# Windowed attention with a routed FFN: values as they lie in memory, 128x64 tiles, and a list planner for the order

## The chip, the cores and the metric

One core of a Trainium2 chip runs the whole program. The metric is the device time of one execution in microseconds. Before the change it is 393.38 us, the median of three runs (390.45 to 393.67).

## The reference

Batch 8, 8 heads, 576 positions, head size 64. Heads 0 to 3 see the last 32 positions, heads 4 to 7 every fourth of the last 128. The joined heads are x of a routed FFN: in each batch the 128 positions with the highest gate score go through a two-layer FFN and get its result added.

```python
scores = scale * np.matmul(q, k.transpose(0, 1, 3, 2))
mask_plain = (rel >= 0) & (rel < window)                                        # window 32
mask_dil = (rel >= 0) & (rel < window * dilation) & (rel % dilation == 0)       # dilation 4
attn = np.exp(scores - max) ; attn = attn / (sum + 1e-09)
x = np.matmul(attn, v)                                # heads joined: 576 x 512 for each batch
...
scores = np.einsum('bsd,d->bs', x, w_gate)
top_idx = np.argpartition(-scores[b], capacity)[:capacity]                      # capacity 128
ye = np.maximum(xe @ w1, 0.0) @ w2                                              # 512 -> 1024 -> 512
out[b, top_idx] = x[b, top_idx] + g[:, None] * ye                               # g: sigmoid of the score
```

## The kernel before

A batch is five units (`UNITS`, line 36): p0 and p1 are 256 positions of the plain heads, d0 and d1 256 of the dilated heads, and l the 64 last positions of both. Queries are grouped by 32; each group sees 64 keys (48 in the dilated half of l). A unit goes through these steps:

1. `scores` (141): 16 matmuls on tiles of 128 rows by 32 columns, 12 in l. A matmul takes two heads at once: queries and keys of two heads lie one under the other in the partitions, and the keys are laid out with zeros so that the heads stay apart. The trace counts each float32 matmul as two instructions, so 32 a unit.
2. `maximum` (153, VectorE): adds the mask, finds the maximum of each head, and subtracts it.
3. `transposes` (176): four 128x128 transposes into one PSUM bank, tile t.
4. `weights` (187, ScalarE): one exponential of 128 x 512 into tile pt.
5. `attend` (197): 16 matmuls (12 in l) again on 128x32 tiles, 130 value columns each, two heads at once. For this the values vp, vd and vl lie in SBUF with zeros between the heads.
6. `normalise` (210): the reciprocal of the sum on VectorE, then the division on ScalarE (8 instructions) or VectorE (1); `store` (234) writes x to memory, `gate` (252, VectorE) takes its dot product with the gate vector.

After a batch's last unit comes the routing: `order` and `spread` (286, 294) add the two halves of the score on TensorE and VectorE and spread them over all partitions; `rank` and `mark` (305, 314, VectorE) count for each position how many are better and mark its slot; `pick` (323) gets the indices by matmul, and POOL fetches the 128 rows by an indirect DMA. `experts` (341) is the FFN: 48 matmuls of 512 columns (three to a product, with both sides split in a rounded part and a rest), turns by TensorE between the layers, and an indirect DMA that writes the rows back. The FFN weights are split in the same way at the start, ScalarE rounding and POOL subtracting (`split_weights`, 276), through four buffers `raw`.

The order is written out in a loop (491 to 533). Iteration g issues the value products of unit g - 2, the scores of g, the division and store of g - 2, the transposes and exponentials of g - 1, half of the iteration's FFN pieces (three or four, `rate`), `maximum` of g and `gate` of g - 2, the routing steps that fall due, and the other FFN pieces. Loads stand at the iteration's end on SP's queue: queries and keys of the next batch behind the scores that read them last, and values of the next batch behind the value products that read them last,

```python
        if 0 <= g - 2 < total and b + 1 < B:
            if u == 2:
                load_vp(b + 1)
                load_vl(b + 1)
            if u == 4:
                load_vd(b + 1)
```

since vp, vd and vl have one buffer each, as have queries and keys. PSUM's eight banks: two for scores (s), one for transposes (t), two for a unit's products (a), three for all the rest (m).

Of the kernel before, what the change touches and what calls it, by code (L numbers as in the profile page):

```python
# [9 lines left out]
F32 = mybir.dt.float32  # L10
# [30 lines left out]
    xd=4,  # L41
    xe=6,
    w1=(2, 4), w2=(7, 9),
    per=2,
    rate=(3, 4, 4),
)


@with_exitstack
def tile_window_attention_moe(ctx, tc, qt, kt, va, vb, w_gate, w1, w2, masks, mask_l, ident, slots, toks, outs, capacity):  # L50
# [6 lines left out]
    ctx.enter_context(tc.manual_schedule())  # L57


    id32 = cp.tile([P, P], F32, name="id32")  # L60
    perm = cp.tile([P, P], F32, name="perm")
# [3 lines left out]
    mkl = cp.tile([P, 2 * LK], BF16, name="mkl")  # L65
# [7 lines left out]
    vp = cp.tile([P, 18, 2, 2 * (D + 1)], F32, name="vp")  # L73
    vd = cp.tile([P, 4, 4, 2, 2 * (D + 1)], F32, name="vd")
    vl = cp.tile([P, 4, 2, 2 * (D + 1)], F32, name="vl")
# [5 lines left out]
    raw = {}  # L81
# [15 lines left out]
    def load_vp(b, lo=0, hi=9):  # L97
        for h in range(2):
            for u in range(2):
                src = va[b, u * GK:(u + 1) * GK, 4 * VW:13 * VW].rearrange("k (c h f) -> k c h f", c=9, h=2)  # L100
                nc.sync.dma_start(  # L101
                    out=vp[h * GK:(h + 1) * GK, 2 * lo:2 * hi].rearrange("k (c u) h f -> k c u h f", u=2)[:, :, u, h],
                    in_=src[:, lo:hi, h])

    def load_vd(b):
        for j in range(4):
            n = GK if j < 3 else G
            for h in range(2):
                src = va[b, G * j:G * j + n, 0:4 * VW].rearrange("k (r h f) -> k r h f", r=4, h=2)[:, :, h]
                nc.sync.dma_start(out=vd[h * GK:h * GK + n, 3 - j, :, h], in_=src)  # L110

    def load_vl(b):
        for h in range(2):
            for i in range(2):
                src = vb[b, i * LK:(i + 1) * LK].rearrange("k (e h f) -> k e h f", e=2, h=2)[:, :, h]
                nc.sync.dma_start(out=vl[h * LK:(h + 1) * LK].rearrange("k (e i) h f -> k e i h f", i=2)[:, :, i, h],  # L116
                                  in_=src)
# [6 lines left out]
    def window(kind, s, c, w):  # L124

        if kind == "p":
            g = 8 * s + 4 * c + w
            return qs[0], G * g, ks[0], G * g, GK, vp[:, g]
        if kind == "l":
            if c:  # L130
                return window("p", 2, 0, w)
            return qs[1], 4 * P + 16 * w, ks[1], SR * w, LK, vl[0:2 * LK, w]
        j = 2 * s + c
        return qs[1], P * w + G * j, ks[1], SR * w + SR - G * (j + 1), GK, vd[:, j, w]

    def chunks(kind):

        return ((4, P, LK, 0), (2, HB, GK, 4 * LK)) if kind == "l" else ((4, P, GK, 0), (4, P, GK, 4 * GK))


    def scores(g):
        kind, s = UNITS[g % NU]
        st = ps.tile([P, 512], F32, tag="s", bufs=2, name=f"s_{g}")
        for c, (nw, rows, wid, o) in enumerate(chunks(kind)):
            for p in range(2):
                for w in range(nw):
                    q, q0, k, k0, _, _ = window(kind, s, c, w)
                    out = st[G * w:G * (w + 1), o + 2 * p * wid:o + 2 * (p + 1) * wid]
                    nc.tensor.matmul(out.rearrange("q (h k) -> q h k", h=2), q[:, p, q0:q0 + G],  # L149
                                     k[:, p, :, k0:k0 + wid], start=True, stop=True)  # L150
        return st

    def maximum(g, st):
        kind, s = UNITS[g % NU]
        ms = wk.tile([P, 512], F32, tag="ms", bufs=3, name=f"ms_{g}")
        mx = wk.tile([P, 8], F32, tag="mx", bufs=3, name=f"mx_{g}")
        for c, (nw, rows, wid, o) in enumerate(chunks(kind)):
            first = s == c == 0
            m = {"p": (mk0 if first else mk)[:, GK:2 * GK], "d": (mk0 if first else mk)[:, 0:GK],
                 "l": mk[:, GK:2 * GK] if c else mkl[:, 0:LK]}[kind]  # L160
            for w in range(4):
                cols = slice(o + w * wid, o + (w + 1) * wid)
                nc.vector.tensor_tensor_reduce(  # L163
                    out=ms[:rows, cols], in0=st[:rows, cols], in1=m[:rows], scale=1.0, scalar=-3.0e38,
                    op0=ALU.add, op1=ALU.max, accum_out=mx[:rows, 4 * c + w:4 * c + w + 1])
        parts = chunks(kind) if kind == "l" else ((8, P, GK, 0),)
        i = 0
        for nw, rows, wid, o in parts:
            n = max(nw, 4)
            v = ms[:rows, o:o + n * wid].rearrange("q (u k) -> q u k", u=n)  # L170
            nc.vector.tensor_tensor(  # L171
                out=v, in0=v, in1=mx[:rows, i:i + n].unsqueeze(2).to_broadcast([rows, n, wid]), op=ALU.subtract)
            i += n
        return ms

    def transposes(g, dt):
        kind, s = UNITS[g % NU]
        tt = ps.tile([P, 512], F32, tag="t", bufs=1, name=f"t_{g}")
        for c, (nw, rows, wid, o) in enumerate(chunks(kind)):
            for p in range(2):  # L180
                t0 = 256 * c + p * rows
                nc.tensor.transpose(tt[:2 * wid, t0:t0 + rows], dt[:rows, o + 2 * p * wid:o + 2 * (p + 1) * wid],  # L182
# [429 lines left out]
```

## Time and profile before

| | |
|---|---|
| time, median of three runs | 393.38 us |
| the profiled execution | 391.99 us, span 390.3 us, mean granted clock 0.85 |
| TensorE busy (matmuls; weight loads) | 276.3 us, 71% of the span; 211.9 us |
| VectorE, ScalarE, POOL busy | 211.7, 107.1, 53.5 us |
| chain that ended last, by engine | PE 34%, DMA 19%, SP's queue 15%, issue 13%, DVE 13% |
| its largest lines | value load vp 12%, value products (line 206) 10%, py (389) 6%, ph (374) 6%, scores (149) 6% |
| value loads of a batch | vp 4 DMAs of 292.5 KB, vd 8 of 130 or 65 KB, vl 4 of 48.8 KB |

PE is TensorE, PEld its weight loads, DVE VectorE, ACT ScalarE, SPq the queue of SyncE, from which nearly all DMAs are issued. The granted clock is a share of 2.4 GHz; the chip knows 2.4 and 1.2 GHz, so a mean of 0.85 is a mixture of both. A line's idle time is that of the engine just before it, with what ended it. Matmuls overlap, so the time from one start to the next tells more than the length of one.

### The profile page before, as it was taken

What the parts mean: (1) busy time and instruction counts of PE and PEld (TensorE: products, weight loads), DVE (VectorE), ACT (ScalarE), POOL (GpSimd) and SP (SyncE); (2) the same over time, 40 slices, a digit from 0 to 9 for tenths busy, and PEclk for the clock granted to TensorE, in tenths of its full rate; (3) what the DMA queues carried; (4) which work ended last, traced back from release to release, by engine and by line L of the source; (5) the groups of instructions that cost most, each with busy time, mean ns of one, the idle gap of its engine ahead of it and who ended that gap; (6) DMA issues with size and microseconds to landing.
All of it is one profiled execution on the core that took longest, in us unless ns stands there. A gap on an engine that the chain in (4) does not pass through costs nothing.

```text
span 390.3 us, 8755 instructions
## 1 busy us (share of the span) xinstructions
PE 276.3 (71%) x3193; PEld 211.9 (54%) x3193; DVE 211.7 (54%) x1173; ACT 107.1 (27%) x346; POOL 53.5 (14%) x59
## 2 busy tenths in 40 slices
PE   6658255596579756796679866795679956788794
PEld 3546144484457555574457654564557644566573
DVE  2439728673574807565384716656384726654631
ACT  1012204343323222241323321241232421252120
POOL 9612502242200100010000100010000100010011
PEclk9997758687688988899688986899888986898999
DMA  7988987789822968259741968149561974112000
GB/s 171 223 207 253 219 182 189 230 223 203 212 67 56 235 124 205 71 154 188 181 111 42 242 134 210 61 117 210 131 178 39 223 141 110 54 39 59 28 27 27
DMA packets 62203, 56.37 MB, mean 144 GB/s; under 512 B 5840, under 2 KB 52176, under 8 KB 62160
## 3 DMA queue, kind: packets, MB, share of 16 engines
q1 hardware_dynamic: 60448, 51.49, 56.8%
q0 software_dynamic: 1280, 4.20, 3.4%
q8 instruction: 25, 0.41, 0.4%
q10 hardware_dynamic: 432, 0.12, 0.2%
q14 instruction: 18, 0.15, 0.1%
HBM read 44.26 MB, written 11.53 MB: 143 GB/s over the span
## 4 chain that ended last, share of the span: by engine, by line
PE 34%; DMA 19%; SPq 15%; issue 13%; DVE 13%; POOL 2%; ACT 2%; POOLq 0%; DVEq 0%
DMA vp<-in_va_dram 12%; PE a L206 10%; PE py L389 6%; PE ph L374 6%; PE s L149 6%; SPq L101 5%; DMA out_dram<-x 4%; SPq L94 3%; DVE ms L163 3%; SPq L116 3%; PE t L182 2%; DVE junk L262 2%; DVE junk L310 2%; DVE ms L171 2%; PE pht L382 2%
## 5 line engine op out<-in xcount | busy, mean ns | idle before, releaser
L230 ACT ACTIVATE x<-a,rin 128x64 f32<-128x64 f32 (+1 forms) x216 | 46.9, 325 | 95.3 <-DVE rin L220 62.9
L206 PE MATMUL a<-vp,pt 128*32 128x130 f32 x576 | 37.5, 370 | 38.6 <-DMA vp<-in_va_dram 22.0
L149 PE MATMUL s<-ks,qs 128*32 128x128 f32 (+1 forms) x1216 | 58.0, 316 | 4.7 <-DMA ks<-in_kt_dram 4.7
L206 PEld LDWEIGHTS a<-vp,pt 128*32 128x32 f32 x576 | 27.3, 149 | 49.3 <-issue 38.6
L149 PEld LDWEIGHTS s<-ks,qs 128*32 128x32 f32 x1216 | 48.3, 130 | 6.9 <-issue 5.4
L163 DVE CUSTOM_DVE_ANT_0 ms<-s,mk 128x64 f32<-128x64 f32 (+1 forms) x288 | 44.5, 218 | 12.1 <-PE s L149 12.1
L262 DVE CUSTOM_DVE_ANT_0 junk<-x,wg 128x256 bf16<-128x256 f32 x80 | 38.4, 480 | 9.3 <-DMA wg<-in_gate_dram 6.2
L218 DVE TENSOR_SCALAR den<-a 128x8 f32<-128x8 f32 (+2 forms) x48 | 7.0, 159 | 62.7 <-PE a L206 62.7
L310 DVE SCALAR_TENSOR_TENSOR junk<-sb,sc,thr_sb 128x576 bf16<-128x576 f32 (+1 forms) x40 | 33.0, 826 | 13.3 <-ACT sb L302 13.3
L192 ACT ACTIVATE pt<-t 128x512 f32<-128x512 f32 (+2 forms) x48 | 24.0, 522 | 53.8 <-PE t L182 53.8
L374 PE MATMUL ph<-w1h,xh 128*128 128x512 f32 x64 | 31.9, 499 | 6.0 <-ACT xh L347 6.0
L336 POOL DMA_INDIRECT xe<-out_dram,ix x8 | 7.9, 991 | 196.8 <-DVE ix L332 196.8
L348 DVE TENSOR_TENSOR hl<-pht,hh 128x512 fp32r<-128x512 f32 x16 | 11.1, 692 | 41.5 <-ACT hh L347 41.5
L182 PE MATMUL t<-id,ms 128*128 128x128 f32 (+2 forms) x160 | 30.7, 318 | 0.2 <-DVE ms L171 0.2
L171 DVE TENSOR_TENSOR ms<-ms,mx 128x512 f32<-128x512 f32 (+2 forms) x48 | 29.6, 630 | 1.1
L389 PE MATMUL py<-w2h,hh 128*128 128x512 f32 x64 | 29.2, 456 | 0.0
L374 PE MATMUL ph<-w1h,xl 128*128 128x512 f32 x64 | 29.0, 453 | 0.0
L374 PE MATMUL ph<-w1l,xh 128*128 128x512 f32 x64 | 28.3, 443 | 0.0
L300 PE MATMUL pa<-id,sc 128*128 128x128 f32 (+1 forms) x40 | 9.0, 351 | 25.5 <-DVE sc L292 25.5
L389 PE MATMUL py<-w2h,hl 128*128 128x512 f32 x64 | 26.5, 414 | 0.0
L389 PE MATMUL py<-w2l,hh 128*128 128x512 f32 x64 | 26.5, 414 | 0.0
L163 DVE DVE_READ_ACCUMULATOR2_ANT mx<- 128x1 f32 (+1 forms) x320 | 26.3, 82 | 0.0
(77 smaller groups left out, 362.4 us busy)
## 6 DMA issues: line engine op xcount, KB each, us to landing
qs<-in_qt_dram SPq DMA_DIRECT2D x15, 576.0 KB, 6.4
ks<-in_kt_dram SPq DMA_DIRECT2D x30, 288.0 KB, 7.1
vp<-in_va_dram SPq DMA_DIRECT2D x28, 292.5 KB, 9.1
vd<-in_va_dram SPq DMA_DIRECT2D x48, 130.0 KB, 3.3
out_dram<-x SPq DMA_DIRECT2D x72, 64.0 KB, 2.8
out_dram<-x SPq DMA_DIRECT2D x16, 256.0 KB, 2.9
raw<-in_w_dram SPq DMA_DIRECT2D x16, 256.0 KB, 3.8
vl<-in_vb_dram SPq DMA_DIRECT2D x32, 48.8 KB, 6.2
```

What stands on the lines that cost most here:

```text
L101: nc.sync.dma_start(out=vp[h * GK:(h + 1) * GK, 2 * lo:2 * hi].rearrange("k (c u) h f -> k c u h f", u=2)[:, :, u, h], in_=src[:, lo:hi, h])
L149: nc.tensor.matmul(out.rearrange("q (h k) -> q h k", h=2), q[:, p, q0:q0 + G], k[:, p, :, k0:k0 + wid], start=True, stop=True)
L163: nc.vector.tensor_tensor_reduce(out=ms[:rows, cols], in0=st[:rows, cols], in1=m[:rows], scale=1.0, scalar=-3.0e38, op0=ALU.add, op1=ALU.m ...
L171: nc.vector.tensor_tensor(out=v, in0=v, in1=mx[:rows, i:i + n].unsqueeze(2).to_broadcast([rows, n, wid]), op=ALU.subtract)
L182: nc.tensor.transpose(tt[:2 * wid, t0:t0 + rows], dt[:rows, o + 2 * p * wid:o + 2 * (p + 1) * wid], id32[:rows, :rows])
L192: nc.scalar.activation(pt[:n, lo:hi], tt[:n, lo:hi], AF.Exp, scale=SCALE)
L206: nc.tensor.matmul(out, pt[:2 * wid, t0:t0 + G], v.rearrange("k h (p f) -> k h p f", p=2)[:, :, p], start=True, stop=True)
L230: nc.scalar.activation(x[:n, c, h, :], av[:n, c, h, 0:D], AF.Copy, scale=rin[:n, c, h:h + 1])
L262: nc.vector.tensor_tensor_reduce(out=junk[:n], in0=x[:n, c].rearrange("q h d -> q (h d)"), in1=wg[:n, 256 * dil:256 * (dil + 1)], scale=UP ...
L310: nc.vector.scalar_tensor_tensor(out=junk[:n], in0=st["sb"][:n], scalar=st["sc"][:n, t:t + 1], in1=thr_sb[:n, o:o + S], op0=ALU.subtract, ...
L374: nc.tensor.matmul(e["ph"], x[:, i, :], w[:, i, n * 512:(n + 1) * 512], start=i == 0 and k == 0, stop=i == 3 and k == 2)
L389: nc.tensor.matmul(e["py"], x[:, i, :], w[:, i, :], start=i == 0 and k == 0, stop=i == 7 and k == 2)
```

## The change

**Values and their products.** The values keep their layout in memory: a row of 260 numbers holds four heads with a one behind each. vp, vd and vl get two buffers each, chosen by the batch's parity. Where a tile of keys serves two query groups, the transposed weights get the zeros: `pts` are three buffers whose zero parts are written once at the start, and an exponential now is four instructions of 64 partitions x 256, each into its part. A product is then 128 keys by 64 queries (a 128x64 tile) for one head and 65 columns.

```diff
     def load_vp(b, lo=0, hi=9):
-        for h in range(2):
-            for u in range(2):
-                src = va[b, u * GK:(u + 1) * GK, 4 * VW:13 * VW].rearrange("k (c h f) -> k c h f", c=9, h=2)
-                nc.sync.dma_start(
-                    out=vp[h * GK:(h + 1) * GK, 2 * lo:2 * hi].rearrange("k (c u) h f -> k c u h f", u=2)[:, :, u, h],
-                    in_=src[:, lo:hi, h])
+        nc.sync.dma_start(out=vp[b % 2][:, lo:hi].rearrange("k c f -> k (c f)"), in_=va[b, :, (4 + lo) * VW:(4 + hi) * VW])
...
-            nc.scalar.activation(pt[:n, lo:hi], tt[:n, lo:hi], AF.Exp, scale=SCALE)
...
+        for u in range(2):
+            for h in range(2):
...
+                nc.scalar.activation(pts[g % 3][GK * u:GK * (u + 1), 2 * h:2 * h + 2, 0:n, u], src, AF.Exp, scale=SCALE)
...
-                    nc.tensor.matmul(out, pt[:2 * wid, t0:t0 + G],
-                                     v.rearrange("k h (p f) -> k h p f", p=2)[:, :, p], start=True, stop=True)
...
+        for y in range(3 if kind == "l" else 4):
...
+            for h in range(4):
+                f = slice(h * (D + 1), (h + 1) * (D + 1))
+                nc.tensor.matmul(at[HB * (y % 2):HB * (y % 2 + 1), y // 2, f],
+                                 pts[g % 3][:, h, y].rearrange("k u q -> k (u q)"), v[:, f], start=True, stop=True)
```

The dilated positions now stand in another order in x, so a store of d is two DMAs and not four, and `order` adds the halves with five matmuls and not two. In unit l all scores have 64 columns.

**Order.** Each step becomes an entry with its engine, a fixed cost in us, the entries that it needs, a due time, the tile size of TensorE, and the buffers that it takes and frees. The planner takes, again and again, the engine that can start first, and on it, among the entries that could start within 0.05 us of the first, the one due earliest; TensorE pays 1.5 us of due time for another tile size. What is written into the program is the order alone.

```diff
+        while n:
+            best = None
+            for eng, ws in ready.items():
...
+                first = min(t for t, _ in cands)
+                t, w = min(((t, w) for t, w in cands if t <= first + 0.05),
+                           key=lambda c: (c[1].due + (self.penalty if c[1].mode not in (None, mode) else 0.0), c[1].n))
+                if best is None or t < best[0]:
+                    best = (t, w)
...
+            v_in[b, "p"] = A("SP", 0.4, lambda b=b: (load_vp(b), load_vl(b)), [old[0], v_in[b - 1, "p"]], d - 8, lag=8.0)
...
+        att[g] = A("PE", 0.75 if kind == "l" else 0.98, lambda g=g: attend(g), [e, v_in[b, "d" if kind == "d" else "p"]],
+                   d + 6, mode=64, takes=[("a", g)], lag=0.1)
...
+        by_vector = g % T["xv"] == 0
```

Here `old[0]` is the last product that read the same buffer, two batches back. Every second unit is divided on VectorE, where it was 13 of 40. A batch's FFN is due 15 us behind its routing. The work ahead of the first unit (masks, zeros, tables) is not known to the planner.

Where rows moved. **SP's queue, second to fourth batch** (L101, L116 and L110 load values, L87 and L94 queries and keys, L239 to L248 store). Before:

```order
L239 DMA out_dram<-x_1118 128x2x256
L87 DMA qs_77<-in_qt_dram 128x1152
L94 DMA ks_79<-in_kt_dram 64x2x576 x2
L239 DMA out_dram<-x_1239 128x2x256
L246 DMA out_dram<-x_1339 64x256
L248 DMA out_dram<-x_1339 16x256 x4
L87 DMA qs_78<-in_qt_dram 128x2x576
L94 DMA ks_80<-in_kt_dram 64x2x576 x2
L101 DMA vp<-in_va_dram 64x9x130 x4
L116 DMA vl<-in_vb_dram 48x2x130 x4
```

And in the change (L199 and L209 load values, L188 and L195 queries and keys):

```order
L342 DMA out_dram<-x_1727 128x2x256
L188 DMA qs_77<-in_qt_dram 128x1152
L195 DMA ks_79<-in_kt_dram 64x2x576 x2
L342 DMA out_dram<-x_1936 128x2x256
L199 DMA vp_82<-in_va_dram 128x2340
L209 DMA vl_86<-in_vb_dram 48x520 x2
L188 DMA qs_78<-in_qt_dram 128x2x576
L195 DMA ks_80<-in_kt_dram 64x2x576 x2
L349 DMA out_dram<-x_2017 64x256
L351 DMA out_dram<-x_2017 16x256 x4
```

The value load of p and l has moved ahead of the second query and key load and of unit l's store, and it now fills a buffer that is read a batch later.

**ACT's queue at the start** (L192 and L288 are exponentials, L282 and L384 round FFN weights, L334 divides). Before:

```order
L192 ACTIVATE pt_216<-t_211 128x512
L192 ACTIVATE pt_271<-t_266 128x512
L192 ACTIVATE pt_347<-t_342 96x256
L192 ACTIVATE pt_347<-t_342 128x128
L192 ACTIVATE pt_418<-t_413 128x512
L282 CAST w1h<-raw_294 128x512
L282 CAST w1h<-raw_296 128x512
L192 ACTIVATE pt_503<-t_498 128x512
```

And in the change:

```order
L384 CAST w1h<-raw_163 128x512
L384 CAST w1h<-raw_165 128x512
L384 CAST w1h<-raw_167 128x512
L384 CAST w1h<-raw_169 128x512
L288 ACTIVATE pt_87<-t_241 64x8x32 x4
L384 CAST w1h<-raw_194 128x512
L288 ACTIVATE pt_88<-t_255 64x8x32 x4
L384 CAST w1h<-raw_224 128x512
L384 CAST w1h<-raw_246 128x512
L384 CAST w1h<-raw_253 128x512
L334 ACTIVATE x_406<-a_338,rin_399 128x64 x8
L288 ACTIVATE pt_89<-t_392 64x2x3x32 x4
```

The first exponentials stood ahead of all weight casts; now four casts stand ahead of the first, and eight ahead of the third.

**TensorE around a routing** (pg is the sum of the scores' halves, pa their spread, ph, pht and py the FFN, a value products, s scores, t transposes). Before:

```order
L374 MATMUL ph_0_1_1579<-w1h,xl_0_1472 128x512
L382 MATMUL pht_0_0_1645<-id_66,h_0_1499 128x128 x4
L289 MATMUL pg_1673<-sd_1157,perm 128x4
L290 MATMUL pg_1673<-sd_1157,perml 64x1
L300 MATMUL pa_0_1678<-id_66,sc_1158 128x128 x4
L300 MATMUL pa_4_1684<-id_66,sc_1158 128x64
L374 MATMUL ph_0_1_1579<-w1h,xh_0_1471 128x512
...
L206 MATMUL a_1707<-vp,pt_1640 32x2x65 x16
L149 MATMUL s_1724<-ks_80,qs_78 32x128 x16
```

And in the change:

```order
L398 MATMUL pg_2302<-sd_1912,perm 128x2 x4
L399 MATMUL pg_2302<-sd_1912,perml 64x1
L512 MATMUL ph_0_0_2248<-w1h,xh_0_2201 128x512
L512 MATMUL ph_0_0_2248<-w1l,xh_0_2201 128x512
L512 MATMUL ph_0_0_2248<-w1h,xl_0_2202 128x512
L274 MATMUL t_2318<-id_66,ms_2073 128x128 x4
L412 MATMUL pa_0_2340<-id_66,sc_1913 128x128 x4
L412 MATMUL pa_1_2341<-id_66,sc_1913 128x64
...
L239 MATMUL s_2360<-ks_80,qs_78 32x128 x16
...
L305 MATMUL a_2394<-vl_85,pt_88 64x65 x8
```

Between pg and pa, which needs pg's sum from VectorE, stand an FFN piece and a unit's transposes where nothing stood; products and scores are no longer next to each other.

## Rows read from the trace of the kernel before

**Rows 1.** Waits of TensorE: in all, how often, the longest (us)
```profile
PE pa L300 <- DVE sc L292: 25.5, 8, 4.6
PE pi L330 <- DVE oh L319: 23.8, 18, 4.0
PE a L206 <- DMA vp<-in_va_dram: 22.0, 9, 4.6
PE a L206 <- DMA out_dram<-x: 15.1, 4, 11.7
```

**Rows 2.** The chain that ended last, one batch: start, length, what
```profile
125.33 0.61 SPq L94
...
128.85 11.43 DMA vp<-in_va_dram
...
140.41 1.69 PE a L206 x25
```

**Rows 3.** Stretches: length, busy PE, PEld, DVE, ACT, POOL, clock, DMA, GB/s
```profile
228.25:273.08 44.83, 33.23 (x400) 25.52 (x401) 24.85 (x145) 13.16 (x46) 1.96 (x2) 0.85 0.62 144
...
249.00:252.00 3.00, 2.95 (x20) 2.15 (x24) 0.85 (x2) 0.59 (x1) 0.97 (x1) 0.53 0.16 33
252.00:267.00 15.00, 14.28 (x222) 11.45 (x215) 9.12 (x57) 5.58 (x21) 0.99 (x1) 0.98 0.57 135
```

**Rows 4.** Instructions of TensorE in order of time: start, length, what
```profile
256.69 0.39 PE L389 MATMUL py<-w2l,hh 128*128 128x512 f32 x1
256.92 0.39 PE L389 MATMUL py<-w2h,hl 128*128 128x512 f32 x1
257.23 1.10 PE L206 MATMUL a<-vd,pt 128*32 128x130 f32 x32
258.16 1.05 PE L149 MATMUL s<-ks,qs 128*32 128x128 f32 x32
259.14 0.66 PE L182 MATMUL t<-id,ms 128*128 128x128 f32 x4
259.56 0.48 PE L389 MATMUL py<-w2h,hh 128*128 128x512 f32 x1
```

**Rows 5.** The weight loads of the same stretch
```profile
257.23 0.83 PEld L206 LDWEIGHTS a<-vd,pt 128*32 128x32 f32 x32 [0.35 <-issue]
...
259.14 0.42 PEld L182 LDWEIGHTS t<-id,ms 128*128 128x128 f32 x4 [0.20 <-issue]
```

**Rows 6.** Exponentials by shape: count, busy us, mean ns, idle before
```profile
L192 ACT ACTIVATE pt<-t 128x512 f32<-128x512 f32 x32 | 19.5, 608 | 49.6 <-PE t L182 49.6
...
L192 ACT ACTIVATE pt<-t 96x256 f32<-96x256 f32 x8 | 3.2, 400 | 4.2 <-PE t L182 4.2
```

**Rows 7.** A division on VectorE, in order of time
```profile
353.67 0.69 DVE L224 TENSOR_TENSOR x<-a,rin 128x512 f32<-128x512 f32 x1
```

**Rows 8.** The matmuls that spread the scores, all batches, by line
```profile
L300 PE MATMUL pa<-id,sc 128*128 128x128 f32 (+1 forms) x40 | 9.0, 351 | 25.5 <-DVE sc L292 25.5
```

**Rows 9.** The start, in order of time, and POOL's weight splits by line
```profile
53.29 2.38 PE L206 MATMUL a<-vp,pt 128*32 128x130 f32 x29 [11.71 <-DMA out_dram<-x]
...
27.81 0.19 POOL L452 CAST toks_sb<-toks 128x5 f16<-128x5 f32 x1 [11.44 <-DMA toks<-in_toks_dram]
...
L283 POOL TENSOR_TENSOR w1l<-raw,w1h 128x512 fp32r<-128x512 f32 x8 | 10.9, 1380 | 22.6 <-ACT w1h L282 22.6
```

**Rows 10.** The end, in order of time
```profile
351.35 1.77 PE L206 MATMUL a<-vd,pt 128*32 128x130 f32 x32
...
371.21 0.60 PE L363 MATMUL px<-id,xe 128*128 128x128 f32 x4
...
384.60 0.39 PE L389 MATMUL py<-w2h,hl 128*128 128x512 f32 x1
```

**Rows 11.** Key loads: count, KB each, median us from issue to landing
```profile
ks<-in_kt_dram SPq DMA_DIRECT2D x30, 288.0 KB, 7.1
```

More of the change, by code (lines that the diff above doesn't have):

```diff
@@ L1 @@
 import math
-from collections import deque
 from contextlib import ExitStack
@@ L40, with __init__ @@
     warm=9,
[L41 to L45, printed above, removed]
-)
+    unit=3.5,
+    route=6.0,
+    ffn=15.0,
+    piece=1.0,
+    switch=1.5,
+    w1=6.0, w2=20.0, each=1.2,
+    xv=2,
+)
+class Work:
+    __slots__ = ("eng", "cost", "fn", "deps", "due", "mode", "takes", "frees", "end", "left", "users", "lag", "n")
+    def __init__(self, eng, cost, fn, deps, due, mode, takes, frees, lag):
+        self.eng, self.cost, self.fn, self.deps, self.due = eng, cost, fn, deps, due
+        self.mode, self.takes, self.frees, self.lag = mode, takes, frees, lag
+        self.end = None
@@ L145, in scores @@
             for p in range(2):
                 for w in range(nw):
[L147 to L153, printed above, removed]
+                    q, q0, k, k0 = window(kind, s, c, w)
@@ L166, in maximum @@
[L166 to L176, printed above, removed]
-        kind, s = UNITS[g % NU]
[L178 to L182, printed above, removed]
-                                    id32[:rows, :rows])
-        return tt
@@ L286, in order, with round_weights, rest_weights @@
+    def round_weights(i):
+        nc.scalar.copy(parts(i)[0], raw[i])
+    def rest_weights(i):
+        hi, lo = parts(i)
+        nc.gpsimd.tensor_tensor(out=lo, in0=raw.pop(i), in1=hi.bitcast(F32), op=ALU.subtract)
     def order(b):
         st = sts[b]
[L288 to L289 removed]
+        pg = st["pg"] = ps.tile([P, 512], F32, tag="m", bufs=BUFS["m"], name=f"pg_{b}")
+        v = st["sd"][:, 0:4].rearrange("q (s c) -> q c s", s=2)
+        o = pg[:, 0:4].rearrange("q (s c) -> q c s", s=2)
+        for c in range(2):
+            for e in range(2):
+                nc.tensor.matmul(o[:, c], perm[:, c, e], v[:, e], start=e == 0, stop=e == 1)
@@ new lines, in experts @@
+        for i in range(8):
+            last = A("PE", 0.7, lambda i=i: ffn2(i), [last, hl[i // 4], wd[8 + i]], d + pc * (11 + i), mode=128,
+                     takes=[("m", ("py", k))] if i == 0 else (), frees=[("e", k)] if i == 7 else (), lag=0.1)
+        y = A("DVE", 0.68, result, [last, gn], d + pc * 19, takes=[("raw", ("y", k))], frees=[("m", ("py", k))])
+        A("POOL", 1.1, put, [y] + stored, d + pc * 19, frees=[("raw", ("y", k)), ("xe", k)])
+    pw = ps.tile([P, 512], F32, tag="m", bufs=BUFS["m"], name="pw")
@@ L537, in _tables @@
+    for t, w in pl.run():
+        w.fn()
 def _tables(nt):
```

530 lines of the change are left out of this document (328 added, 202 removed).

## The prediction

> **What bounds the kernel now.** I read four views. First the waits of TensorE [rows 1]: four rows hold 86.4 us of its idle time, 37.1 before value products (the value loads; the rows that name a store end at the same place, behind the same queue) and 49.3 inside the routing, where the small matmuls wait for VectorE. Then one batch of the chain [rows 2]: a value load takes 11.43 us and the next thing is a value product. It starts so late because values have one buffer: it can only be issued after the last product that reads the batch before. Third, the stretches [rows 3]: a batch takes 44.83 us, in which TensorE is busy 33.23 and VectorE 24.85, at a granted clock of 0.85 of 2.4 GHz. In the 15 us without either wait TensorE is busy 14.28 and the clock is 0.98; just before, behind a routing wait, it is 0.53, that is, nearly all at 1.2 GHz. So the kernel has no engine that is full: waits bound it, and each wait costs twice, once as idle time and once as a lower clock after it. Last, the instructions in order of time at full clock [rows 4, 5], for prices.
>
> **Prices on TensorE at 2.4 GHz, start to start** [rows 4]: one FFN matmul 0.23, a unit's value products 0.93, scores 0.98, transposes 0.42, and 0.31 instead of 0.23 where an FFN matmul is followed by products, so 0.08 for a change of tile size.
>
> **Value products on 128x64 tiles.** The count stays at 32 instructions a unit (24 in unit l), the columns streamed over each tile halve, the tiles are two and not four. No row shows the new form. Below: 0.93, if two tiles overlap as well as four do. Above, or rather what I take: the weight loads. 32 loads of 32 columns take 0.83, four of 128 columns 0.42 [rows 5], both 0.81 to 0.82 ns a column one after the other, so 32 loads of 64 columns take 1.66, and with the 0.10 by which the products now exceed their loads 1.76 (unit l 1.32). The order of the new loop speaks for it as well: four heads in a row go to the same 64 columns. 1.76 is nearer to the rows, since both load rows give the same price a column. It adds 0.83 x 32 + 0.61 x 8 = 31 us of TensorE over the kernel. The Trainium skill, "TensorEngine Tiling (Array Packing)", Theoretical Speedup, gives up to two times for 64 columns and four for 32; half the columns on half the tiles would then cost the same 0.93, and the 31 us would be nothing. The load rows speak against it.
>
> **Order: more changes of tile size.** 132 in place of 82, at 0.08 each 4 us, on the path. The page above, Key Properties, says that a change of mode drains the engine; if each waited out a matmul in flight (about 0.3 here, an estimate), the sum would rise by some 29 us. The 0.31 against 0.23 says that it doesn't.
>
> **Value loads.** Two buffers a kind and one DMA for vp instead of four (vl 2 for 4, vd 4 for 8). In SP's new order the load for batch b+2 stands right behind the last reader of batch b, a batch ahead of its use; 11.43 us [rows 2] fits into a batch three times. So the 25.4 us of steady value waits (37.1 less the 11.7 of the first batch) go. Bytes are the same.
>
> **Exponentials.** Four instructions of 64 x 256 for one of 128 x 512. The nearest row, 96 x 256, takes 0.40 against 0.61 [rows 6]; four are at most 1.6, so ACT gains 1.0 a unit, 5 a batch, less what it saves because 20 units instead of 27 are divided there. ACT is busy 13.2 of 44.8 now and at most 18 of some 32 after: hidden, but 1 us longer in each unit's chain. The l unit's wider masks, the five small matmuls for two and the zeroing of weights before the start go with it, under 1 us a batch, beside other work.
>
> **VectorE** gains 1.5 divisions a batch at 0.69 [rows 7]: 24.85 + 1.0 = 25.9.
>
> **TensorE's sum for a batch**: scores 4 x 0.95 + 0.71 = 4.5; products 4 x 1.76 + 1.32 = 8.4; transposes 2.1; FFN 48 x 0.23 = 11.0; three turns 1.3; spreading the scores 9.0 / 8 = 1.1 [rows 8], other routing 0.5 (estimate, a few matmuls of the same kind); 16.5 changes x 0.08 = 1.3. Together 30.2. So TensorE and VectorE are now nearly equal, and what is late next is whichever of the two the other waits for.
>
> **Start, to the products of unit 5** (now at 53.29 [rows 9]). POOL splits weights only after the 27.81 us copy that waits for a table; 19 DMAs stand ahead of that table instead of 31, so some 22. But ACT's new order puts four weight casts ahead of the first exponential and twelve ahead of unit 5's, and weights go through four buffers, each freed by a POOL split of 1.38. Twelve tiles at about 2 us each from 24 on: unit 5's exponentials at 48, its products at 51. Ends: 45 (at POOL's 1.38 each), 60 (3 us each). The gain of the load there is eaten by the casts.
>
> **Body, the 34 units from there to the last products.** 6.8 batches x 30.2 = 205; three units' scores are already done (-2.8); and the new order lets the FFN lag: 2.5 of 8 stand behind the last products, so 5.5 run in this stretch and not 6.8, and 1.3 of 12.3 leave (-16): 186 on TensorE, at most 176 on VectorE. What share of the time TensorE is busy I bound by 0.95 (the 15 us without waits) and 0.74 (the whole batch, 33.23 of 44.83) [rows 3]. The value wait is gone, but VectorE rises from 0.61 of that clean stretch to over 0.9 of TensorE's work: I take 0.86. 186 / 0.86 = 217; ends 196 and 251.
>
> **Tail.** Now 390.3 - 351.35 = 39.0. After: products 1.8, turn and half an FFN 5.9, routing 0.8, two FFNs of 13.8 each, turn to last matmul (371.21 to 384.99), then 5.3 to the end [rows 10]: 41. The last batch's routing hides beside the first of them.
>
> **Query and key loads** keep one buffer, now with a value load of 1.2 MB ahead of them. A load needs about 9 (7.1 to land [rows 11] and three issues at 0.61 [rows 2]); between the last reader and the next, the new order has 11 to 13 us of TensorE work. I put 3 us in all, ends 0 and 28 (2 us at each of 14 reloads).
>
> **Sum:** 51 + 217 + 41 + 3 = 312 of span, and 1.7 around it as now (391.99 less 390.3): 314. The profiled execution lies 1.4 under the median of 393.38; I add nothing for that. From the other side: 392 - 25 (value waits) - 2 (start) - 45 (routing waits but the last) + 31 + 4 + 2 = 357, were the clock as it is. TensorE's 276.3 busy us hold about 211 of work at full clock (8 x 25.8, which is the sum above with products as before and 82 changes, and the warm-up), so 65 are low clock; 314 has 43 of them back.
>
> **Rivals.**
> - *Products as cheap as before* (0.13). Speaks for it: columns times tiles are equal. Then TensorE has 160 in the body, and VectorE's 176 bounds: 176 / 0.86 = 205, so 302.
> - *The clock stays low* (0.14). The idle gaps of routing remain in part (the matmul that spreads scores stands one or two FFN pieces behind the one that makes them, with VectorE between), or query and key loads arrive late 14 times by 2 us, and after each the clock is at 1.2 GHz as in the 0.53 row. The other sum: 357, or 345 with a fifth of the 65 back.
> - *Slower: the two engines take turns* (0.05). Both work in order, by a list made from fixed costs (0.98 for products that I price at 1.76); one late piece holds all behind it, on both. If nothing overlaps, the body is 186 + 176 = 362, and with the 97 of the other terms 459. It decides where less than 0.38 of VectorE's work is hidden; at 0.3 the body is 186 + 0.7 x 176 = 309 and the time 406. Against it: even now, with a fixed order, 33.23 + 24.85 - 44.83 = 13.3 of 24.85 is hidden, 0.53; at that share the time is 186 + 0.47 x 176 + 97 = 366.
> - *The loads are not early* (0.02), if SP is held by a store that waits: the 25 come back, 339.
>
> **Numbers.** Forecast 0.66. A measurement here tells 1% from no change. Forecast, cheap products, low clock, late loads and most of turn-taking short of its point are faster: 0.93; slower 0.05, the point itself 0.02. The range takes the forecast's bounds together with the cheap products and part of the low clock: under 290 needs 0.95 in the body and the early start (0.08), over 350 the unchanged clock or turn-taking (0.12).
>
> **What would show it.** Right: no TensorE wait on value loads after the first batch, products at 1.7 to 1.8 a unit with weight loads of about 52 ns, clock above 0.93, 6.0 to 6.8 us from product to product in the body, first ACT exponential behind four casts. Wrong: products near 0.95; a clock near 0.85; TensorE rows that wait on ks or qs; VectorE under 0.6 busy while TensorE waits for it.

## The result

The changed kernel takes 320.72 us, median of four runs (317.03 to 323.25), against 393.52 for the kernel before, median of four (390.45 to 396.31): ratio 0.814, 95% interval 0.803 to 0.825. Here and below, medians and ranges are of all runs of a kernel, and ratios to the kernel before leave out runs over 1.5% slower than the fastest of the same kernel. The profiled execution is the run of 317.03, with a span of 314.4. The forecast was 314, the range 290 to 350. So the sum is 2% under the median, but, as the trace and the experiments show, its step on the start failed, its products and its busy share were mis-sized, and the errors nearly cancel.

### The profile page after: what moved, and what is told of

Read it like the earlier page. It is cut to its first block, busy times and chain, and to the rows that moved or that the text cites. A ratio compares the mean times of both kernels' runs of the same rounds, so it can differ in the third digit from the quotient of the medians.

```text
span 314.4 us, 8768 instructions
## 1 busy us (share of the span) xinstructions
PE 264.9 (84%) x3241; PEld 209.5 (67%) x3241; DVE 209.1 (67%) x1184; ACT 132.1 (42%) x402; POOL 50.1 (16%) x61
## 4 chain that ended last, share of the span: by engine, by line
PE 40%; issue 32%; DMA 19%; SPq 3%; DVE 2%; POOL 2%; ACT 1%; POOLq 1%
PE a L305 11%; DMA ks<-in_kt_dram 9%; PE s L239 8%; PE ph L512 6%; PE py L533 6%; DMA vd<-in_va_dram 5%; PE t L274 4%; DMA vp<-in_va_dram 4%; PE pg L398 2%; DMA raw<-in_w_dram 2%; POOL xe L461 1%; DVE ms L253 1%; PE pa L412 1%; PE pht L521 1%; SPq L204 1%
## 5 line engine op out<-in xcount | busy, mean ns | idle before, releaser
L288 ACT ACTIVATE pt<-t 64x256 f32<-64x256 f32 (+1 forms) x160 | 58.8, 368 | 45.4 <-PE t L274 27.1
L239 PE MATMUL s<-ks,qs 128*32 128x128 f32 x1216 | 47.5, 299 | 7.2 <-DMA ks<-in_kt_dram 3.6
L253 DVE CUSTOM_DVE_ANT_0 ms<-s,mk 128x64 f32<-128x64 f32 (+1 forms) x288 | 44.4, 217 | 12.0 <-PE s L239 9.4
L239 PEld LDWEIGHTS s<-ks,qs 128*32 128x32 f32 x1216 | 37.3, 120 | 16.5 <-issue 9.2
L274 PE MATMUL t<-id,ms 128*128 128x128 f32 (+1 forms) x160 | 27.5, 294 | 22.7 <-ACT pt L288 22.7
L334 ACT ACTIVATE x<-a,rin 128x64 f32<-128x64 f32 (+1 forms) x160 | 34.8, 327 | 25.7 <-PE a L305 9.0
L274 PEld LDWEIGHTS t<-id,ms 128*128 128x128 f32 (+1 forms) x160 | 20.0, 149 | 30.3 <-ACT pt L288 23.9
L305 PE MATMUL a<-vp,pt 128*64 128x65 f32 x576 | 32.5, 238 | 0.5 <-issue 0.5
L305 PEld LDWEIGHTS a<-vp,pt 128*64 128x64 f32 x576 | 29.2, 147 | 5.2 <-issue 4.1
L305 PEld LDWEIGHTS a<-vd,pt 128*64 128x64 f32 x512 | 23.5, 142 | 11.1 <-issue 7.7
L305 PE MATMUL a<-vd,pt 128*64 128x65 f32 x512 | 25.7, 233 | 6.0 <-ACT pt L288 3.8
L533 PE MATMUL py<-w2h,hh 128*128 128x512 f32 x64 | 29.2, 457 | 0.3 <-ACT hh L467 0.3
L512 PE MATMUL ph<-w1h,xl 128*128 128x512 f32 x64 | 25.4, 397 | 0.0
L533 PE MATMUL py<-w2h,hl 128*128 128x512 f32 x64 | 25.4, 396 | 0.0
```

Source lines behind the costliest of these rows:

```text
L239: nc.tensor.matmul(st[G * w:G * (w + 1), c, p], q[:, p, q0:q0 + G], k[:, p, :, k0:k0 + GK], start=True, stop=True)
L253: nc.vector.tensor_tensor_reduce(out=ms[:rows, c, p, h], in0=st[:rows, c, p, h], in1=m[:rows], scale=1.0, scalar=-3.0e38, op0=ALU.add, op1 ...
L274: nc.tensor.transpose(tt[:, p, c, :rows], dt[:rows, c, p].rearrange("q h k -> q (h k)"), id32[:rows, :rows])
L288: nc.scalar.activation(pts[g % 3][GK * u:GK * (u + 1), 2 * h:2 * h + 2, 0:n, u], src, AF.Exp, scale=SCALE)
L305: nc.tensor.matmul(at[HB * (y % 2):HB * (y % 2 + 1), y // 2, f], pts[g % 3][:, h, y].rearrange("k u q -> k (u q)"), v[:, f], start=True, s ...
L334: nc.scalar.activation(x[:n, c, h, :], av[:n, c, h, 0:D], AF.Copy, scale=rin[:n, c, h:h + 1])
```

## The profile after

The waits of TensorE, which answer to [rows 1] (instruction, what it waited for: us in all, times, longest):

```profile
PE t L274 <- ACT pt L288: 22.7, 5, 13.3
PE a L305 <- ACT pt L288: 3.8, 1, 3.8
PE s L239 <- DMA ks<-in_kt_dram: 3.6, 3, 2.0
...
PE pi L447 <- DVE oh L437: 1.5, 2, 0.9
```

No row names a value load, the row on sc (25.5 before) is gone and the one on oh is 1.5 instead of 23.8. What is left lies nearly all before 100 us, where transposes wait for ScalarE to have an exponential done. The stretches, cut at the products of unit 5, at 100 us and at the last products, against [rows 3] (start and end, length, busy PE, PEld, DVE, ACT, POOL, granted clock, DMA share, GB/s):

```profile
0.00:61.95 61.95, 32.46 (x494) 25.21 (x494) 26.58 (x191) 21.48 (x55) 29.58 (x42) 0.92 0.90 254
61.95:100.00 38.05, 29.11 (x422) 24.58 (x422) 27.27 (x161) 15.69 (x48) 5.65 (x5) 0.78 0.90 235
100.00:270.03 170.03, 166.76 (x2129) 131.56 (x2127) 138.40 (x786) 85.41 (x277) 10.02 (x10) 1.00 0.64 175
270.03:314.40 44.37, 36.54 (x200) 28.17 (x200) 16.84 (x48) 9.57 (x24) 4.90 (x5) 0.96 0.14 42
```

From 100 us to the last products TensorE is busy 166.76 of 170.03 us at the full clock: there it is the bound, and VectorE (0.81) follows. Before 100 us it is not, and the DMA engines are at 0.90. The start is to be read on ScalarE, on SP and at unit 5's products, in order of time, against [rows 9]:

```profile
23.92 2.56 ACT L384 CAST w1h<-raw 128x512 fp32r<-128x512 f32 x4 [21.62 <-DMA raw<-in_w_dram]
26.38 1.58 ACT L288 ACTIVATE pt<-t 64x256 f32<-64x256 f32 x4
...
36.56 1.30 ACT L384 CAST w1h<-raw 128x512 fp32r<-128x512 f32 x2 [4.83 <-DMA raw<-in_w_dram]
...
48.01 0.62 ACT L384 CAST w2h<-raw 128x512 fp32r<-128x512 f32 x1 [6.51 <-DMA raw<-in_w_dram]
...
54.15 1.29 ACT L384 CAST w2h<-raw 128x512 fp32r<-128x512 f32 x2 [3.92 <-DMA raw<-in_w_dram]
...
58.66 1.59 ACT L288 ACTIVATE pt<-t 64x256 f32<-64x256 f32 x4
```
```profile
18.89 9.12 SPq L376 DMA_DIRECT2D raw<-in_w_dram  x6
28.07 0.42 SPq L199 DMA_DIRECT2D vp<-in_va_dram  x1
...
29.53 2.39 SPq L376 DMA_DIRECT2D raw<-in_w_dram  x3
...
32.91 3.05 SPq L195 DMA_DIRECT2D ks<-in_kt_dram  x2
...
36.64 3.58 SPq L204 DMA_DIRECT2D vd<-in_va_dram  x4
```
```profile
61.95 1.55 PE L305 MATMUL a<-vp,pt 128*64 128x65 f32 x32
```

The first exponential stands behind four casts, as forecast, and later casts wait for weights (6.51 us before the one at 48.01) while the second batch's values have gone into the same queue at 28 and 36. The first of these are read at 61.95, by unit 5, and vd at 93.70. The products and their weight loads at full clock, which answer to [rows 4] and [rows 5]:

```profile
161.87 1.55 PE L305 MATMUL a<-vp,pt 128*64 128x65 f32 x32
163.34 0.50 PE L512 MATMUL ph<-w1h,xh 128*128 128x512 f32 x1
...
165.04 0.39 PE L512 MATMUL ph<-w1h,xl 128*128 128x512 f32 x1
165.36 1.55 PE L305 MATMUL a<-vp,pt 128*64 128x65 f32 x32
```
```profile
161.87 1.41 PEld L305 LDWEIGHTS a<-vp,pt 128*64 128x64 f32 x32 [0.20 <-ACT pt L288]
```

A unit's products take 1.48 us start to start (1.47 from 161.87 to 163.34, 1.48 in most others), not 1.76; their 32 loads take 1.41, that is 44 ns each. A change of size costs what was forecast: 0.32 from the FFN matmul at 165.04 to the products.

## The experiments

Theory at this point: early loads take away 25 us of waits, the planned order takes away the routing waits and with them the low clock, and the new tiles cost time. The edits below take these apart. "The loop" is the written-out order of the kernel before, "planned" that of the change.

### Early loads in the kernel before

```
-    vp = cp.tile([P, 18, 2, 2 * (D + 1)], F32, name="vp")
+    vp = [cp.tile([P, 18, 2, 2 * (D + 1)], F32, name=f"vp{i}") for i in range(2)]
...
-            if u == 2:
+            if u == 0:
                 load_vp(b + 1)
+            if u == 2:
                 load_vl(b + 1)
```

Only vp gets a second buffer and moves; vl and vd are loaded where they were. Room for vp came from one buffer fewer of ms, mx, x and raw.

> The kernel before, with two buffers for the pair values and its value loads issued two units earlier in the same written-out order; tiles and order unchanged. Theory (the waits for value loads cost their idle time and a lower clock after it): the 25.4 us of steady waits go, and part of the low clock with them, 350 to 367 us; no TensorE wait on vp after the first batch, clock above 0.87. Rival (the order alone earns the change, and the routing waits take over what the loads leave): 380 to 393 us, with the idle time moved to the rows that wait for VectorE.

Measured: 367.94 (366.12 to 370.48), ratio 0.942 (0.932 to 0.952). The waits of TensorE:

```profile
PE pa L300 <- DVE sc L292: 29.2, 8, 4.6
PE pi L330 <- DVE oh L319: 22.8, 17, 4.0
PE s L149 <- DMA ks<-in_kt_dram: 11.4, 4, 5.8
...
PE a L206 <- DMA vp<-in_va_dram: 0.8, 1, 0.8
```

25 us less, 1 us above the theory's range. It is not simply the 25.4 us of the sum: the value waits fell from 37.1 to 0.8, and others rose (keys from 4.7 to 11.4, the routing's pa from 25.5 to 29.2). TensorE's idle time, span less busy time, fell by 19 us (114.0 to 95.0), and the same 3193 instructions kept it busy 269.4 us instead of 276.3. A steady batch, from the first products of the fifth batch to those of the sixth, before and here:

```profile
183.65:228.25 44.60, 33.32 (x398) 25.48 (x399) 24.85 (x145) 13.15 (x46) 1.97 (x2) 0.85 0.63 145
```
```profile
174.89:213.97 39.08, 31.19 (x399) 23.91 (x398) 24.79 (x146) 12.96 (x47) 1.97 (x2) 0.87 0.71 165
```

It is 5.5 us shorter: 3.4 of idle time and 2.1 of busy time, at a clock of 0.87 instead of 0.85. So the wait cost clock as well, if less than the theory had it: over the whole span the mean clock is 0.828, below the 0.87 expected, because it is 0.61 from 30 to 60 us (0.70 before).

### One value buffer in the changed kernel

```
-        nc.sync.dma_start(out=vp[b % 2][:, lo:hi]...
+        nc.sync.dma_start(out=vp[0][:, lo:hi]...
...
-            old = [att[NU * (b - 2) + i] for i in (2, 4)] if b > 1 else [None, None]
+            old = [att[NU * (b - 1) + i] for i in (2, 4)]
```

vd and vl likewise; the planner makes its order anew from these dependences.

> The changed kernel with one buffer for each kind of values, so that the load of a batch waits again for the last reader of the batch before; new tiles and planned order stay. Theory (early loads are needed): 317 + 25 to 37, 342 to 355 us, with TensorE waits on vp of some 3 to 5 us a batch. Rival (the planned order has enough FFN work to stand in the gap, so the loads' earliness is worth little once the order is planned): 317 to 325 us.

Measured: 310.22 (309.40 to 313.60), ratio 0.794 (0.784 to 0.805): neither; it is faster than the change (0.814, with an interval that just touches this one). There is no TensorE wait on values in it either. The place in SP's queue and the distance to the reader explain it. SP and TensorE of this kernel in order of time:

```profile
194.03 0.64 SPq L188 DMA_DIRECT2D qs<-in_qt_dram  x1
194.72 1.24 SPq L195 DMA_DIRECT2D ks<-in_kt_dram  x2
196.06 0.54 SPq L199 DMA_DIRECT2D vp<-in_va_dram  x1
```
```profile
193.92 0.79 PE L305 MATMUL a<-vl,pt 128*64 128x65 f32 x13
...
194.73 0.45 PE L305 MATMUL a<-vp,pt 128*64 128x65 f32 x5
...
215.32 1.55 PE L305 MATMUL a<-vp,pt 128*64 128x65 f32 x32
```

And in the kernel before:

```profile
216.19 2.73 SPq L101 DMA_DIRECT2D vp<-in_va_dram  x4
```
```profile
208.31 0.27 PE L206 MATMUL a<-vp,pt 128*32 128x130 f32 x1
...
226.96 0.39 PE L206 MATMUL a<-vp,pt 128*32 128x130 f32 x2 [3.34 <-DMA vp<-in_va_dram]
```

The load goes out at 196.06, 0.9 us after unit l, the last reader of vp, has ended (195.18), and its next reader comes at 215.32, 19 us on, because FFN pieces stand between the units. In the kernel before the same load went out 7.6 us behind its last reader (216.19 after 208.58) and was needed 7.4 us later (226.96 less the wait of 3.34). A second buffer was not needed once the order was planned. What one buffer gains is nearly all in the start: of the 5.8 us between the profiled spans (314.4 and 308.6), 5.1 are there by unit 5's products, at 56.87 instead of 61.95. There the second batch's values go out at 43, behind most of the weights, and not at 28.

### New tiles in the loop, loads late and early

Both take layout, tiles, masks and exponentials from the change and the order of the work from before; both have two buffers for values, and they differ in the units at which values are loaded (u == 2 and 4, or u == 0 and 2).

```
         if 0 <= g - 2 < total and b + 1 < B:
-            if u == 2:
+            if u == 0:
                 load_vp(b + 1)
                 load_vl(b + 1)
-            if u == 4:
+            if u == 2:
                 load_vd(b + 1)
```

> The new layout, tiles and masks in the written-out loop of the kernel before, value loads at its places (late). Theory (tiles cost, order and loads earn): products at 1.48 for 0.93 a unit add 32 x 0.55 + 8 x 0.4 = 21 us, fewer and larger value loads give a little back: 400 to 415 us. Rival (the new tiles and layout earn something by themselves, through 16 fewer VectorE divisions and a third of the packets): 375 to 393 us.

> As the kernel with the new tiles in the written-out loop, with the value loads two units earlier, into two buffers. Theory (value waits cost 25 us and some clock): 25 to 40 us below its twin with late loads, 365 to 385 us; what then remains to the changed kernel's 317 is the planned order. Rival (the fixed order keeps TensorE at the routing waits, loads early or not): within 8 us of its twin.

Measured: late 377.14 (375.68 to 380.50), ratio 0.965 (0.952 to 0.977); early 372.20 (367.33 to 376.45), 5 us below its twin, 8 in the profiled executions (spans of 375.8 and 367.7). The theory missed both, and the rivals came nearer: tiles and layout together did not cost, and early loads earned 5 to 8 and not 25. The late kernel's waits tell why:

```profile
PE pa L414 <- DVE sc L407: 27.6, 8, 5.4
PE pi L449 <- DVE oh L439: 23.5, 18, 3.9
PE a L307 <- DMA vp<-in_va_dram: 11.7, 3, 8.7
```

Value waits are 11.7, not 37.1 [rows 1], at the old places of the loads, and all three stand before 134 us. From the fifth batch on a batch takes 41.0 us in either kernel, so early loads earn only in the first ones. SP spends 0.59 and 0.89 us on the issues of vp and vl of a batch where it spent 2.73 and 5.03 (one DMA and two, not four and four). The load still leaves 7.3 us behind its last reader (208.14 after 200.82), but the next one comes 9.9 us after that, at 218.08, where it was needed after 7.4. How much of this is due to fewer DMAs, and how much to the longer products and exponentials in between, no run separates.

In all, TensorE's idle time fell by 18.6 us (114.0 to 95.4). It is busy 280.4 us, only 4 more than before, although the dearer products should add 21 (the expectation's estimate); some 17 us of its busy time must have come back, at a mean clock of 0.88 for 0.85. I had booked "Bytes are the same" and given the number of DMAs no price of its own.

### Routing spread out in the loop

```
-        add(g0 + 1, lambda: (spread(b), gather_scores(b)))
+        add(g0 + 2, lambda: (spread(b), gather_scores(b)))
...
-            add(g0 + 1 + (t > 2), lambda t=t: rank(b, t))
+            add(g0 + 2 + (t > 2), lambda t=t: rank(b, t))
...
-                add(g0 + 1 + (t > 2), lambda s=s, t=t: mark(b, s, t))
+                add(g0 + 2 + (t > 2), lambda s=s, t=t: mark(b, s, t))
...
-            add(g0 + 2, lambda s=s: (pick(b, s), number(b, s), fetch(b, s)))
-            add(g0 + 3, lambda s=s: ffn.extend(experts(b, s)))
+            add(g0 + 4, lambda s=s: (pick(b, s), number(b, s), fetch(b, s)))
+            add(g0 + 5, lambda s=s: ffn.extend(experts(b, s)))
```

> The kernel with the new tiles in the written-out loop and early loads (372.20), with the routing's steps set further apart: the matmul that spreads the scores one unit after the one that makes them, the picking two units after the ranks, the FFN two units later than before. Nothing else changes; no planner. Theory (the planner earns by putting TensorE's work into the routing's VectorE time, and the clock follows): a batch of 41.00 us with TensorE busy 32.65 falls to 33 to 35, the waits on sc and oh (50 us) nearly vanish, the clock goes above 0.93, and the time to 320 to 335 us, the tail taking back some 4. Rival (the fixed loop keeps TensorE and VectorE in step unit by unit, and the idle time comes back before other instructions): 355 to 372 us.

Measured: 340.99 (338.36 to 344.36), ratio 0.877 (0.868 to 0.886). One batch of its twin with early loads, and one of this kernel:

```profile
181.50:222.50 41.00, 32.65 (x405) 25.70 (x405) 25.02 (x146) 17.58 (x60) 1.97 (x2) 0.92 0.56 160
```
```profile
150.00:184.99 34.99, 31.21 (x405) 24.60 (x405) 24.30 (x146) 17.52 (x61) 1.97 (x2) 1.00 0.65 186
```

And what TensorE waits for in this kernel:

```profile
PE px L499 <- DMA xe<-out_dram,ix: 19.1, 7, 8.4
PE a L307 <- ACT pt L290: 16.7, 15, 4.7
```

The same 405 instructions in 34.99 instead of 41.00 us, at a clock of 1.00 instead of 0.92. The waits on sc and oh, 50 us in the twin, are gone from the rows, and the low clock of a batch is gone with them. So five lines of the order are worth 25 to 28 us (the medians lie 31 apart, but the kernel before took 389.66 beside this one and 392.96 beside its twin). But 341 is above the 335 expected at most: of the idle time some came back, 19.1 us at px and 16.7 at the exponentials (1.4 and 9.8 in the twin). px waits for the gathered rows: POOL's fetch now starts 5.7 us behind the picking (223.68 after 217.97), where it started 0.6 behind it (190.74 after 190.10). The theory holds for about half of the planner's share; how much of the rest the rival's idle time makes up is not shown.

### The start: weights later

```
-            o = A("SP", 0.1, lambda i=i: load_weights(i), (), d, ...)
-            o = A("ACT", 0.62, lambda i=i: round_weights(i), [o], d + 6)
...
+        for i in range(2 * g, 2 * g + 2) if nt and g < 8 else ():
+            o = A("SP", 0.1, lambda i=i: load_weights(i), [att[g]], d, ...)
+            o = A("ACT", 0.62, lambda i=i: round_weights(i), [o], d + 12)
```

> The changed kernel with the loads, casts and splits of the FFN weights tied to the attention units (two tiles a unit, the casts due twelve units' microseconds later), so that the first exponentials stand ahead of all casts; value buffers stay two. Theory (in the start the ordered casts hold the exponentials, and weights hold the queue): the first transposes no longer wait 13.3 us for an exponential, the products of unit 5 end at 45 to 50 instead of 61.95, and the time is 305 to 310 us. Rival (the start is bound by the bytes that the transfers must move, 254 GB/s over the first 62 us whatever the order): unit 5 stays at 58 to 62, and the time at 316 to 321.

Measured: 321.66 (319.01 to 324.03), ratio 0.816 (0.810 to 0.822): no gain. Its waits of TensorE (its profiled run, 324.03, is 2 us above the median):

```profile
PE s L239 <- DMA ks<-in_kt_dram: 24.7, 6, 5.9
PE t L274 <- ACT pt L288: 7.6, 5, 2.1
```

The wait of 13.3 behind the casts is gone, as the theory said, and unit 5 comes at 55.72. But scores now wait 24.7 us for keys instead of 3.6: the casts were only the last thing in line, and the transfers of the first batches are behind them. The rival was right on the time, to 1 us, and 2 us too late with unit 5; the theory's 45 to 50 was further off.

> Both edits to the changed kernel: one buffer for each kind of values, and the FFN weights tied to the units. Theory (one buffer earned 7 us because the value load of the second batch no longer stands between weights and the second batch's keys; that is the same cost that later weights remove): the two do not add up, 302 to 308 us. Rival (they are two costs, of the queue and of ScalarE): 296 to 301 us, with the products of unit 5 before 47 us. A second rival (late weights make the first FFN late, and TensorE idles for it): above 310.

Both edits together: 310.02 (307.55 to 317.34), ratio 0.787 (0.779 to 0.794), which these runs cannot tell from one buffer alone (310.22, 0.794). They do not add up; the median is 2 us above the 302 to 308 that I expected for that case, and two of the four runs lie inside.

### The order of the two column tiles

```
-        for y in range(3 if kind == "l" else 4):
+        ny = 3 if kind == "l" else 4
+        for y, h in [(y, h) for y0 in (0, 2) for h in range(4) for y in range(y0, min(y0 + 2, ny))]:
...
-            for h in range(4):
```

y picks the half of the columns. The change issues four heads (eight instructions) on one half and then four on the other; this edit alternates.

> The changed kernel with the value products issued so that the two column tiles alternate (head by head, first one half of the columns, then the other) instead of four heads in a row on one tile. Theory (weight loads follow each other at one price a column, so the order of tiles does not matter): products stay at 1.45 to 1.55 us a unit, and the time at 315 to 322 us. Rival (four in a row queue on one tile, and alternating lets two tiles overlap): products at 0.95 to 1.2 us a unit, 0.3 to 0.5 x 40 units = 12 to 20 us less of TensorE, which is full from 100 us on: 300 to 308 us.

Measured: 309.41 (306.91 to 310.58), ratio 0.788 (0.783 to 0.793): the rival's products, and its time within 1.5 us. TensorE and the loads of one unit, and the loads of a unit l, where the last eight instructions have one half to themselves:

```profile
161.46 1.15 PE L305 MATMUL a<-vp,pt 128*64 128x65 f32 x32
162.55 1.05 PE L398 MATMUL pg<-sd,perm 128*128 128x2 f32 x8
```
```profile
161.46 1.01 PEld L305 LDWEIGHTS a<-vp,pt 128*64 128x64 f32 x32 [0.35 <-issue]
...
168.51 0.55 PEld L305 LDWEIGHTS a<-vl,pt 128*64 128x64 f32 x16 [0.37 <-issue]
168.97 0.54 PEld L305 LDWEIGHTS a<-vp,pt 128*64 128x64 f32 x8
```

1.09 us a unit instead of 1.48, by order alone. So weight loads have no fixed price a column: loads of 64 columns come 68 ns apart where one tile has all of them (0.54 / 8), 44 where four heads in a row share it (1.41 / 32), and 32 to 34 where the tiles alternate (1.01 / 32 and 0.55 / 16). Whether the load itself or the product behind it on the same tile sets this, no run separates. My theory of the products fell here.

### Together, and more buffers for weights

> The changed kernel with one value buffer and the alternating column tiles, weights early as in the change. If the two edits add up (310.22 and 309.41 against about 319): 299 to 303 us. If VectorE or the transfers at the start take over: 304 to 310.

> One value buffer, later weights and alternating column tiles together. If the column order does not matter: the time of its twin without alternation, within 2 us. If it does: 12 to 20 us below that twin, unless VectorE (busy 209 us of work, 25 of 30 us in the middle) then bounds, which would leave 5 to 10.

> The one-buffer, alternating kernel with eight instead of four buffers for arriving FFN weights, in the room of the second value buffers; the planner then sets nearly all weight loads ahead of the second batch's queries and keys. Theory (the start is bound by bytes in SP's order, so weights loaded earlier push queries and keys later): 2 to 8 us slower than its twin with four. Rival (the start is held by buffers that come free late, which stop SP): 2 to 6 us faster.

One buffer with alternation: 305.58 (300.71 to 308.59), ratio 0.778 (0.770 to 0.787), inside the 304 to 310 expected if something else takes over. The sum of both gains would be a ratio of 0.768, which these intervals hardly tell from 0.778. TensorE is then busy 151.17 of the 155 us from 100 on, the start is that of one buffer alone (unit 5 at 57.24 for 56.87), and the waits for keys are 13.2 us instead of 7.5.

With later weights as well: 306.81 (303.12 to 309.29), ratio of the medians 0.780, no difference that these runs can tell, though unit 5 comes at 48.10. That is 3 us below the same kernel without alternation, neither the 12 to 20 of the expectation nor the 5 to 10 that VectorE would leave.

With eight weight buffers instead of four: 311.21 (310.05 to 311.97), 5.6 above its twin, as the theory said. Its products of unit 5 come at 60.74 instead of 57.24, and the longest wait for an exponential is 16.1 us instead of 13.4: weights sent earlier bring eight casts instead of four ahead of the first exponentials. So more buffers, in the order that the planner makes with them, do not shorten the start, and neither sending weights earlier nor later than the change does shortens the whole.

## Why the prediction was right, and where it was not

**Value loads: the waits went, but two buffers were not what it needed.** In the kernel before, early loads are worth the 25 us that the sum says; that the two agree is in part luck, since 36 us of value waits went and other waits rose. "Two buffers a kind ... So the 25.4 us of steady value waits ... go" names a cause that was not needed: under the planned order one buffer has no value wait either, and in the loop with the new layout none is left from the fifth batch on, even with late loads. What early loads earn depends on what the order leaves to earn: 25 us in the kernel before, 5 to 8 with the new tiles in the loop, and about -8 in the planned one (ratio 0.814 against 0.794).

**"Each wait costs twice": right in kind, too high in size.** When the routing waits were moved, the clock of a batch came back from 0.92 to 1.00; the batch lost 4.6 us of idle time and 1.4 of busy time. When the value waits went, the clock came back only from 0.85 to 0.87, with 3.4 us of idle and 2.1 of busy time. So a us of idle time was worth 1.3 and 1.6 us, not 2. The forecast of over 0.93 held in the profiled execution: 0.951, and 1.00 from 100 us on; the four runs show 0.951, 0.899, 0.914 and 0.957.

**Products: 1.76 forecast, 1.48 measured (loads of 44 ns, not 52); the failed premise is "the same price a column".** Two rows at one price, [rows 5], were not a law: loads of 64 columns took 0.5, 0.7 and 1.1 ns a column by the order of their tiles. Why those of 32 and 128 columns agree at 0.8, no run shows. The sentence that four heads in a row go to the same columns was the better half of the argument, since that order costs 0.39 of the 1.48. The rule named there, up to two times for 64 columns (the Trainium skill, "TensorEngine Tiling (Array Packing)", Theoretical Speedup), fits the alternating order: 68 ns alone against 34 in the same unit l is 2.0 times. The rival with cheap products was within reach of an edit of the loop, and at 1.09 against 0.93 still not quite there.

**Start: the step that failed.** Forecast 51 with an upper end of 60, measured 61.95. (Its own terms would give ends of 24 + 12 x 1.38 + 3 = 44 and 24 + 12 x 3 + 3 = 63.) "Twelve tiles at about 2 us each from 24 on" had the casts in the right place, twelve ahead of unit 5's exponentials. But the twelfth ends at 55.44 and not at 48, 2.6 us a tile, above all because three casts waited for weights to land (4.83, 6.51 and 3.92 us), with the DMA engines at 0.90 for the first 100 us. And unit 4's exponentials and a division stand between the twelfth cast and unit 5's exponentials at 58.66, 3.2 us that the sum left out. I had priced POOL's splits and ScalarE's casts and not the transfers; and I saw the second values' early load only as a gain, though in this stretch it stands between the weights and the keys. One buffer removes 5 us of the miss; holding the weights back shifts it to the keys. What a better start would be worth stays open: the loop with the new tiles reaches unit 5's products at 41.06 (early loads) and 40.16 (spread routing), and by 100 us TensorE has run 851 and 912 instructions there, no more than the 914 of the change.

**Body: 217 forecast, 220 with the 3 for the keys, 208.1 measured** (61.95 to 270.03). The 6.1 a unit lie inside the 6.0 to 6.8 named only as an average: the first five units take 8.1 each (to 102.23), the other 29 take 5.8. Two terms were mis-sized and cancel in part. Cheaper products take some 9 off the 186, yet TensorE is busy 195.9 us, as 38 us of the body lie at a clock of 0.78; and the share of 0.86 was too low, 195.9 / 208.1 = 0.94. VectorE is the bound in no stretch above: from 100 us on it is busy 0.81 beside a full TensorE. Taking turns, the slower rival, has nothing for it in the rows.

**Tail 44.4 for 41, keys 3.6 for 3, change of size 0.09 for 0.08.** Against the 312 of span the errors are +11 in the start, -12 in the body with the keys, +3 in the tail; they nearly cancel, which is luck.

**Where the 73 us come from**, in steps that were run, each set against the kernel before beside it: new tiles and layout in the loop -14 to -16 (what the dearer products cost is paid within it), early loads -5 to -9, routing set apart -25 to -28, and the rest of the planner some -24. These steps were taken in one order; early loads show that another order gives other shares. What the planner does in its last 24 us was not taken apart: the 19.1 at px and 16.7 at the exponentials in the kernel with spread routing are where it can be.

## What to carry to other kernels

Price a wait by the order of the work and not only by its buffers: ask how long after the last reader a load leaves, and how much work stands before the next reader; a second buffer is worth only what is left. On split tiles of TensorE, look at the order in which the tiles are issued before the price of a load, and let neighbours go to different tiles. In the start, add up the bytes in queue order first; casts and splits that seem to hold it may only be waiting in the same line, and a milestone reached earlier (one unit's products) need not shorten the whole.

## What the runs showed of the hardware that I had not expected

- Loads and products of different column tiles pass one another in the records: in unit l of the changed kernel all sixteen instructions on vl are issued before the eight on vp, yet the trace has them mixed from the fourteenth on:

```profile
86.89 1.30 PE L305 MATMUL a<-vl,pt 128*64 128x65 f32 x13 [1.30 <-DVE x L328]
87.88 0.37 PE L305 MATMUL a<-vp,pt 128*64 128x65 f32 x1
87.98 0.32 PE L305 MATMUL a<-vl,pt 128*64 128x65 f32 x1
```

- The granted clock of the start differs between executions of nearly the same work (only the order of the column tiles differs), 494 matmuls in each: 0.73 with one buffer, 0.97 in its alternating twin.

```profile
0.00:56.87 56.87, 30.91 (x494) 23.82 (x494) 27.93 (x191) 21.45 (x55) 30.17 (x42) 0.73 0.84 240
```
```profile
0.00:57.24 57.24, 30.41 (x494) 22.68 (x494) 27.70 (x191) 21.80 (x56) 30.20 (x42) 0.97 0.84 238
```

TensorE is busy 30.91 and 30.41 us in them, and unit 5's products come at the same time. So a lower mean clock here cost the matmuls next to nothing: the mean of a stretch counts its idle time too, and only the busy time beside it tells what the clock cost.
